# Merging the rest tiles, summing squares ahead of the router product, and re-timing GpSimd in an attention and expert kernel

## The chip, the cores and the metric

The kernel runs on one core of a Trainium2 chip. The metric is the device time of one launch in microseconds (us). The engines named here are TensorE (PE; its weight loads are the row PEld), VectorE (DVE), ScalarE (ACT), GpSimd (POOL) and SyncE (SP), which issues most transfers. Each engine works through its own list of instructions in order and waits on semaphores for the others.

## The reference, cut to what matters

Attention over 8 batches of 12 heads, 448 positions, head size 64, whose softmax has one more term in the denominator; then a router that sends each of the 448 tokens of a batch to one of 8 experts, and a two-layer expert.

```
scores = q @ k.T / sqrt(64);  m = max(scores);  e = exp(scores - m)
attn   = e / (sum(e) + exp(-m) + 1e-9);   attn_out = attn @ v
x      = attn_out, heads side by side                  # (8*448, 768)
xn, en = x / (norm(x) + 1e-6), expert_emb / (norm(expert_emb) + 1e-6)
logits = xn @ en.T / tau;  expert_idx = argmax(logits);  gate = softmax(logits)[expert_idx]
out    = gate * (relu(x @ w1[expert_idx]) @ w2[expert_idx])
```

## The kernel before: the parts that the change touches

The work is cut into 48 groups (six pairs of heads in each of eight batches). A group's 448 keys are three blocks of 128 and a "rest" of 64. The rests of the pair's two heads share one matmul. Every piece of work is put at a position; positions are sorted, and each engine gets its instructions in that order. A slot is 8 positions; group `g` begins at `8*g`. One slot thus mixes the scores of group `g`, the product with V of group `g-1`, the transposes for group `g+1`, and, once they run, two or three pieces ("chunks") of an expert of an earlier batch.

```python
LAG = 2 * NP                        # NP = 6; experts of batch b begin LAG groups after its first group
FILL = ((2.8, 5.3, 5.4), (2.8, 5.4))   # positions of expert chunks in even and odd slots, 15 a batch
...
def front_qk(k, g, s):              # transposes: q and k of a pair, one tile of two banks
    ps = k.big.tile([128, 2, 512], F32, name="big", tag="big")
    for m, x, r in ((0, t.qm, t.qr[...]), (1, t.km, t.kr[...])):
        for j in range(3):
            nc.tensor.transpose(ps[:, m, 128 * j : 128 * j + 128], x[:, j, ...], k.ident[:])
        nc.tensor.transpose(ps[:, m, SM:512], r, k.ident[:])      # the rest, one for q and one for k
    k.put(s + 1.1, k_out)           # ScalarE copies the 512 columns of k
    k.put(s + 2.1, q_out)           # VectorE copies the 448 columns of q
...
def scores(k, g, j, pa, pv):        # j = 0, 1, 2: a block of keys; j = 3: the rests, in a "work" tile
    ...                             # at pa: ScalarE takes exp; at pv: VectorE subtracts 1
def attend(k, g, s):                # product with V, in the one "av" tile: rests first, then 6 matmuls
    ...
    k.put(s + 2.3, recip)           # ScalarE: Ln, then Exp(-1 * .), gives 1 / denominator
def normalise(k, g, s): ...         # VectorE: x = (av + sum of v) * that
def square(k, g):                   # x*x: GpSimd for the first 11 groups, ScalarE after
    ...
def router_mm(k, b, s):             # 3 rounds of 4 column strips: 2 strips x@en, 2 strips sum of squares
    for r in range(3):
        for q in range(4): ...
def router_tok(k, b, s): ...        # 4 transposes of the router's result, in a "big" tile
...
    put(s + 1.2, lambda n=n: sum_v(k, n))                         # GpSimd: three adds every second group
    for j, o, pa, pv in ((0, 0, .3, 1.5), (1, .05, .4, 2.6), (2, 5.2, 6, 7.7), (3, .15, 2.6, 7)):
        put(s + o, lambda ...: scores(k, g, j, s + pa, s + pv))
    put(s + 8 + 0.1, lambda ...: attend(...)); put(s + 8 + 4.75, lambda ...: normalise(...))
    put(-NSLOT, lambda: warm(k, 24))                              # matmuls that keep TensorE busy at the start
...
n.work = pool("work", 2, space=PSUM)   # 2 tiles of one bank, taken in turn
n.big = pool("big", 2, space=PSUM)     # 2 tiles of two banks, taken in turn
n.av = pool("av", 1, space=PSUM)       # 1 tile of two banks
```

Expert chunks take "work" tiles as well: 8 of the hidden layer and 7 of the output, emptied by ScalarE or VectorE. After a batch's router, its most frequent expert is read into a register and GpSimd issues seven loads of that expert's weights.

Of the kernel before, what the change touches and what calls it, by code (L numbers as in the profile page):

```python
# [21 lines left out]
NP = H // 2  # L22
NF = F // 128
SM = 384
SR = S - SM
GP = 2
NG = 3
LAG = 2 * NP
FILL = ((2.8, 5.3, 5.4), (2.8, 5.4))
NSLOT = 8  # L30
# [6 lines left out]
def build_consts(k):  # L37
    nc, pool = k.nc, k.const
    nc.scalar.preload_act_table_set("natural_log_exp_and_others")
    k.ident = pool.tile([128, 128], F32, name="ident")  # L40
    make_identity(nc, k.ident[:])
    k.ones_f = pool.tile([128, 1], F32, name="ones_f")
    nc.vector.memset(k.ones_f[:], 1.0)
    iota_i = pool.tile([128, E], I32, name="iota_i")
    nc.gpsimd.iota(iota_i[:], pattern=[[1, E]], base=0, channel_multiplier=0)
    row_i = pool.tile([128, 1], I32, name="row_i")
    nc.gpsimd.iota(row_i[:], pattern=[[0, 1]], base=0, channel_multiplier=1)
    k.row = pool.tile([128, 1], F32, name="row")
    nc.vector.tensor_copy(out=k.row[:], in_=row_i[:])
    k.iota = pool.tile([128, E], F32, name="iota")  # L50
    nc.vector.tensor_copy(out=k.iota[:], in_=iota_i[:])

    k.vld, k.krest, k.qrest, k.vab = [], [], [], []
    for s in range(NG):
        v = pool.tile([128, 2 * GP, 4, DH], F32, name=f"vld{s}")
        nc.gpsimd.memset(v[:, :, 3, :], 0.0)
        k.vld.append(v)
        kr = pool.tile([128, GP, 128], F32, name=f"krest{s}")
        nc.vector.memset(kr[:], 0.0)
        k.krest.append(kr)  # L60
        qr = pool.tile([128, 2 * GP, DH], F32, name=f"qrest{s}")
        nc.gpsimd.memset(qr[64:128, :, :], 0.0)
        k.qrest.append(qr)
    for s in range(2):
        va = pool.tile([128, 4, 3, 64], F32R, name=f"vab{s}")
        nc.vector.tensor_copy(out=va[:, :, 1, :], in_=k.ones_f[:, 0:1].unsqueeze(2).broadcast_to([128, 4, 64]))
        k.vab.append(va)


# [66 lines left out]
def load_qk(k, n):  # L136

    nc = k.nc
    b, h0 = n // NG, n % NG * 2 * GP
    g0, s = h0 // 2, n % NG  # L140
    t = Net()
    t.qm = k.qkp.tile([128, 3, 2 * GP, DH], F32, name="qm", tag="qm")
    t.km = k.qkp.tile([128, 3, 2 * GP, DH], F32, name="km", tag="km")
    t.kr, t.qr, t.v = k.krest[s], k.qrest[s], k.vld[s]

    def rest2(src, two):
        return src[b].rearrange("(g two) s d -> two s g d", two=2)[two, SM:S, g0 : g0 + GP, :]

    keng = nc.sync if n else nc.scalar
    for eng, dst, src in ((nc.sync, t.qm, k.q), (keng, t.km, k.k)):  # L150
        for j in range(3):
            eng.dma_start(
                dst[:, j, :, :], src[b, h0 : h0 + 2 * GP, 0:SM, :].rearrange("h (p t) d -> t p h d", t=3)[j]
            )
    nc.sync.dma_start(t.qr[0:64, :, :], k.q[b, h0 : h0 + 2 * GP, SM:S, :].rearrange("h p d -> p h d"))
    keng.dma_start(t.kr[0:64, :, 0:64], rest2(k.k, 0))
    keng.dma_start(t.kr[64:128, :, 64:128], rest2(k.k, 1))
    k.ld[n] = t
# [14 lines left out]

def sum_v(k, n):

    nc, t = k.nc, k.ld[n]
    vs = k.vsp.tile([128, 2 * GP, DH], F32, name="vs", tag="vs")
    nc.gpsimd.tensor_tensor(out=vs[:], in0=t.v[:, :, 0, :], in1=t.v[:, :, 1, :], op=ALU.add)
    nc.gpsimd.tensor_tensor(out=vs[:], in0=vs[:], in1=t.v[:, :, 2, :], op=ALU.add)
    nc.gpsimd.tensor_tensor(out=vs[:], in0=vs[:], in1=t.v[:, :, 3, :], op=ALU.add)  # L180
    k.va[n] = vs


def front_qk(k, g, s):
    nc = k.nc
    n, i = g // GP, g % GP
    t = k.ld[n]
    ps = k.big.tile([128, 2, 512], F32, name="big", tag="big")
    for m, x, r in ((0, t.qm, t.qr[:, 2 * i : 2 * i + 2, :]), (1, t.km, t.kr[:, i, :])):
        for j in range(3):  # L190
            nc.tensor.transpose(ps[:, m, 128 * j : 128 * j + 128], x[:, j, 2 * i : 2 * i + 2, :], k.ident[:])  # L191
        nc.tensor.transpose(ps[:, m, SM:512], r, k.ident[:])  # L192
    def k_out():
        kt = k.qt.tile([128, 512], F32R, name="kt", tag="kt")
        nc.scalar.copy(out=kt[:], in_=ps[:, 1, :])  # L195
        k.kts[g] = kt

    def q_out():
        qt = k.qt.tile([128, S], F32R, name="qt", tag="qt")
        nc.vector.tensor_copy(out=qt[:], in_=ps[:, 0, 0:S])  # L200
        k.qts[g] = qt
    k.put(s + 1.1, k_out)
    k.put(s + 2.1, q_out)

# [9 lines left out]
def scores(k, g, j, pa, pv):  # L214
# [23 lines left out]
    def less_one(e):  # L238
        if j < 3:
            em = k.emp.tile([128, 2, S], F32R, name="em", tag="em")  # L240
            nc.vector.tensor_scalar_sub(em[:], e[:], 1.0)  # L241
        else:
            em = k.emp.tile([128, S], F32R, name="emx", tag="emx", bufs=2)
            nc.vector.tensor_scalar_sub(em[:], e[:, 0, :], 1.0)
        k.ems[g, j] = em
# [4 lines left out]
def attend(k, g, s):  # L250
# [4 lines left out]
    for h in range(2):  # L255
# [3 lines left out]
        )  # L259
    for j in range(3):  # L260
        for h in range(2):
            nc.tensor.matmul(  # L262
                ps[:, h, 0:S], lhsT=va[:, j, h : h + 2, :], rhs=k.ems[g, j][:, h, :],
                start=False, stop=(j == 2),
            )

    i = g % GP
    nc.tensor.matmul(ps[:, 0, S : S + 1], lhsT=k.va[g // GP][:, 2 * i : 2 * i + 2, :], rhs=k.ones_f[:], start=True, stop=True)  # L268
    rd = k.rdp.tile([128, 2, S], F32, name="rd", tag="rd")
    k.avs[g] = ps, rd  # L270

    def recip():
        nc.scalar.activation(rd[:], ps[:, :, 0:S], ACT.Ln, bias=1.0, scale=1.0 / (S + 1.0))  # L273
        nc.scalar.activation(rd[:], rd[:], ACT.Exp, scale=-1.0)  # L274

    k.put(s + 2.3, recip)

# [19 lines left out]


def square(k, g):
    x = k.xs[g]  # L300
    xs = k.xsp.tile([128, S], F32, name="xs", tag="xs")
    if g < LAG - 1:
        k.nc.gpsimd.tensor_tensor(out=xs[:], in0=x[:], in1=x[:], op=ALU.mult)  # L303
    else:
        k.nc.scalar.activation(xs[:], x[:], ACT.Square)
    k.xs[g] = (x, xs)


def router_mm(k, b, s):

    nc = k.nc
    ps = k.big.tile([128, 512], F32, name="rmm", tag="big")
    for r in range(3):
        for q in range(4):
            c = 3 * (q % 2) + r
            x = k.xs[b * NP + c][q // 2]
            nc.tensor.matmul(  # L317
                ps[32 * q : 32 * q + 32, 0:S], lhsT=(k.en[:, c, :] if q < 2 else k.ones32[:]), rhs=x[:],
                start=(r == 0), stop=(r == 2),
            )  # L320
# [5 lines left out]
def router_tok(k, b, s):  # L326

    nc, p = k.nc, k.rp
    tp = k.big.tile([128, 4, 128], F32, name="tok", tag="big")
    for t in range(4):  # L330
# [4 lines left out]
def router_logits(k, b, tp):  # L335

    nc, p = k.nc, k.rp
    nrm = p.tile([128, 4], F32, name="nrm", tag="nrm")
    nc.vector.reduce_sum(out=nrm[:], in_=tp[:, :, 64:128:32], axis=AX.X)  # L339
    l = p.tile([128, 4, E], F32, name="l", tag="l")  # L340
    nc.vector.reduce_sum(
        out=l[:], in_=tp[:, :, 0:64].rearrange("p t (q r) -> p t r q", q=2)[:, :, 0:E, :], axis=AX.X
    )
# [288 lines left out]
def pipeline(k):  # L632
# [6 lines left out]

    k.put = put  # L640
    put(4.6, lambda: build_late_consts(k))
    put(4, lambda: prep_expert_emb(k, 4))
    put(5 * NSLOT + 2.7, lambda: prep_expert_emb_t(k, 5 * NSLOT + 2.7))
    for n in range(NG * B):
        s = n * GP * NSLOT
        put(max(-NSLOT, s - 6 * NSLOT + 5.2), lambda n=n: load_qk(k, n))
        put(max(-NSLOT, s - 5 * NSLOT + 1.1), lambda n=n: load_v(k, n))
        put(s + 1.2, lambda n=n: sum_v(k, n))
    for g in range(G):
        s = g * NSLOT  # L650
        put(s - NSLOT + 4.2, lambda g=g, s=s - NSLOT + 4.2: front_qk(k, g, s))
        put(s + 0.8, lambda g=g: front_v(k, g))
        for j, o, pa, pv in ((0, 0, 0.3, 1.5), (1, 0.05, 0.4, 2.6), (2, 5.2, 6, 7.7), (3, 0.15, 2.6, 7)):
            put(s + o, lambda g=g, j=j, pa=s + pa, pv=s + pv: scores(k, g, j, pa, pv))
# [3 lines left out]
        put(s + 4.75, lambda g=g, s=s: normalise(k, g, s + 4.75))  # L658
        put(s + 7.1, lambda g=g: square(k, g))
    put(-NSLOT, lambda: warm(k, 24))  # L660
    for g in range(LAG):
        for o in (2.8, 5.4):
            put(g * NSLOT + o, lambda: warm(k, 3))
    for b in range(B):
        s = ((b + 1) * NP + 1) * NSLOT
        put(s + 2.75, lambda b=b, s=s: router_mm(k, b, s + 2.75))
        put(s + 7.9, lambda b=b, s=s: router_tok(k, b, s + 7.9))
        s += NSLOT
        put(s + 0.16, lambda b=b: router_pick(k, b))
        put(s + 0.9, lambda b=b: router_pow(k, b))  # L670
        put(s + 3.5, lambda b=b: router_count(k, b))
        put(s + 4.3, lambda b=b: router_index(k, b))
        for i, o in enumerate((4.4, 10, 16, 25, 31, 37, 43)):
            put(s + o, lambda b=b, i=i: fetch(k, b, i))
        put(s + 4.5, lambda b=b: router_exp(k, b))
        put(s + 7.2, lambda b=b: router_act(k, b))
        s += NSLOT
        put(s + 3.5, lambda b=b: keep_rows(k, b))
        put(s + 5.5, lambda b=b: keep_xb(k, b))
        put(s + 6, lambda b=b, s=s: router_gate(k, b, s + 6))  # L680

    late = {2.8: (4.7, False), 5.3: (7.3, True), 5.4: (8.5, True)}
    for b in range(B):
        pos = [((b * NP + LAG + i) * NSLOT, o) for i in range(NP) for o in FILL[i % 2]]
        for (s, o), fn in zip(pos, moe_chunks(k, b), strict=True):
# [7 lines left out]
def kernel(  # L693
# [35 lines left out]
    n.xp = pool("xp", 7)  # L729
    n.xsp = pool("xsp", 6)  # L730
    n.xbp = pool("xbp", 3)
# [3 lines left out]
    n.hp = pool("hp", 10)  # L735
    n.yp = pool("yp", 5)
    n.ld, n.qts, n.kts, n.ems, n.va, n.sv = {}, {}, {}, {}, {}, {}
# [40 lines left out]
```

The softmax here doesn't subtract the row's maximum and nothing guards it: scores larger than these inputs give would overflow.

## Time and profile before

| what | value |
|---|---|
| time, median of 3 | 430.42 us (430.19 to 431.25) |
| profiled span | 430.1 us |
| PE busy | 400.0 us (93%) |
| DVE busy | 314.8 us (73%) |
| ACT busy | 305.3 us (71%) |
| POOL busy | 171.7 us (40%) |
| matmuls | 2430 |

The shares are averages over three stages: attention alone, attention with experts, and the last two batches' experts alone. A row of a timeline has the start, the duration, the engine, the source line with the operation and its tiles, and in brackets how long the engine had been idle and what ended that. In the view of waits a line has the engine and what it wanted, what released it, and then the total, the count and the longest wait. An idle engine costs time only if the work that ends last hangs on it.

### The profile page before, as it was taken

The page shows a single profiled execution, that of the slowest core. Times are in us where ns is not written, and L with a number is a line of the kernel's source. Part 1 is how long each engine was busy: PE and PEld are TensorE (multiplying, and loading weights), DVE is VectorE, ACT ScalarE, POOL GpSimd, SP SyncE. Part 2 cuts the span into 40 slices and gives each one's busy share as a digit, 9 for nine tenths or more (in the row PEclk, how much of TensorE's full clock was granted, in tenths as well). Part 3 has the DMA queues.
Part 4 walks back from the last instruction along what each step waited for, and adds up shares of the span by engine and source line. Part 5 has one row for each costly group of instructions (what it writes and reads, how often), then busy time and mean ns, then how long its engine had stood idle before and what let it go on. Part 6 is the DMA issues. An engine that isn't in the chain of part 4 may idle for free.

```text
span 430.1 us, 7384 instructions
## 1 busy us (share of the span) xinstructions
PE 400.0 (93%) x2430; PEld 248.1 (58%) x2430; DVE 314.8 (73%) x658; ACT 305.3 (71%) x440; POOL 171.7 (40%) x242
## 2 busy tenths in 40 slices
PE   8878987879999999999999999999999999998885
PEld 3555554646556656665666656665666566644443
DVE  1697878789689769887787868976988778754222
ACT  1777776777788977978788878897698878751111
POOL 4043315754359106740377024910675037504500
PEclk9998999899999999999999999999999999999999
DMA  8775552997489964998399938997499508853973
GB/s 168 175 179 123 131 128 65 179 181 158 99 173 216 257 164 96 232 198 232 81 232 199 254 96 152 218 240 198 79 230 203 170 2 135 160 131 52 231 141 130
DMA packets 133690, 69.76 MB, mean 162 GB/s; under 512 B 99849, under 2 KB 127497, under 8 KB 133649
## 3 DMA queue, kind: packets, MB, share of 16 engines
q1 hardware_dynamic: 115392, 43.63, 40.0%
q0 software_dynamic: 16384, 25.17, 34.6%
q10 hardware_dynamic: 1872, 0.46, 0.6%
q8 instruction: 20, 0.33, 0.3%
q14 instruction: 22, 0.17, 0.1%
HBM read 83.39 MB, written 16.52 MB: 232 GB/s over the span
## 4 chain that ended last, share of the span: by engine, by line
PE 56%; DVE 20%; ACT 11%; issue 5%; POOL 4%; DMA 3%; POOLq 1%; DVEq 0%; ACTq 0%
PE av L262 11%; PE work L513 10%; PE work L485 8%; PE big L222 7%; DVE x L286 5%; PE big L191 4%; PE rmm L317 4%; DVE em L241 4%; DVE qt L200 4%; ACT e L233 3%; ACT rd L274 3%; DMA w<-in_moe_w_dram 3%; ACT rd L273 3%; PE work L629 2%; PE work L532 2%
## 5 line engine op out<-in xcount | busy, mean ns | idle before, releaser
L233 ACT ACTIVATE e<-big 128x896 f32<-128x896 f32 x144 | 127.6, 921 | 32.1 <-PE big L222 31.4
L241 DVE TENSOR_SCALAR em<-e 128x896 fp32r<-128x896 f32 x144 | 96.9, 687 | 7.2 <-ACT e L233 6.8
L286 DVE SCALAR_TENSOR_TENSOR x<-av,rd 64x448 f32<-64x448 f32 x96 | 66.3, 691 | 46.7 <-ACT rd L274 36.4
L485 PE MATMUL work<-xb,w 128*128 128x448 bf16 x384 | 79.7, 353 | 1.3 <-DMA w<-in_moe_w_dram 0.8
L262 PE MATMUL av<-em,vab 128*128 128x448 f32 x288 | 73.1, 391 | 0.0
L513 PE MATMUL work<-w,h 128*128 128x384 bf16 x384 | 68.4, 326 | 4.8 <-DMA w<-in_moe_w_dram 2.0
L222 PE MATMUL big<-qt,kt 64*128 64x448 f32 x288 | 56.8, 435 | 15.8 <-DVE qt L200 15.0
L357 POOL TENSOR_TENSOR nrm<-nrm,half 128x4 f32<-128x4 f32 x8 | 8.5, 1068 | 134.0 <-DVE nrm L339 134.0
L262 PEld LDWEIGHTS av<-em,vab 128*128 128x128 f32 x288 | 51.5, 192 | 16.2 <-issue 13.1
L485 PEld LDWEIGHTS <-w 128*128 128x128 bf16 x384 | 34.9, 98 | 39.4 <-issue 9.8
L273 ACT ACTIVATE rd<-av 128x896 f32<-128x896 f32 x48 | 44.1, 919 | 17.4 <-PE av L268 11.2
L445 POOL DMA_DIRECT2D w<-in_moe_w_dram x56 | 45.2, 809 | 27.0 <-issue 23.0
L513 PEld LDWEIGHTS <-h 128*128 128x128 bf16 x384 | 35.5, 98 | 31.5 <-issue 9.3
L222 PEld LDWEIGHTS big<-qt,kt 64*128 64x128 f32 x288 | 24.3, 184 | 43.1 <-ACT e L233 14.4
L200 DVE CAST qt<-big 128x448 fp32r<-128x448 f32 x48 | 29.9, 624 | 24.1 <-ACT kt L195 22.8
L274 ACT ACTIVATE rd<-rd 128x896 f32<-128x896 f32 x48 | 45.7, 952 | 1.5
L195 ACT CAST kt<-big 128x512 fp32r<-128x512 f32 x48 | 28.1, 585 | 12.1 <-PE big L192 12.0
L503 DVE TENSOR_SCALAR y<-work,g 128x384 f32<-128x384 f32 x32 | 19.6, 614 | 15.4 <-PE work L513 11.2
L629 PE MATMUL work<-ident 128*128 128x512 bf16 x96 | 28.6, 426 | 2.0 <-POOL ident masks.py:199 1.7
L493 DVE TENSOR_SCALAR h<-work 128x448 bf16<-128x448 f32 x40 | 24.6, 617 | 6.8 <-PE work L485 6.7
L209 DVE CAST vab<-vld 128x512 fp32r<-128x512 f32 x48 | 29.4, 612 | 0.0
L303 POOL TENSOR_TENSOR xs<-x 128x448 f32<-128x448 f32 x11 | 10.3, 933 | 40.5 <-DVE x L286 34.7
(103 smaller groups left out, 569.2 us busy)
## 6 DMA issues: line engine op xcount, KB each, us to landing
w<-in_moe_w_dram POOLq DMA_DIRECT2D x24, 512.0 KB, 7.9
w<-in_moe_w_dram POOLq DMA_DIRECT2D x32, 384.0 KB, 7.8
qm<-in_q_dram SPq DMA_DIRECT2D x72, 128.0 KB
vld<-in_v_dram SPq DMA_DIRECT2D x24, 384.0 KB
out_dram<-y SPq DMA_DIRECT2D x48, 192.0 KB
km<-in_k_dram SPq DMA_DIRECT2D x69, 128.0 KB
qrest<-in_q_dram SPq DMA_DIRECT2D x24, 64.0 KB
vld<-in_v_dram SPq DMA_DIRECT2D x48, 32.0 KB
```

What stands on the lines that cost most here:

```text
L200: nc.vector.tensor_copy(out=qt[:], in_=ps[:, 0, 0:S])
L222: nc.tensor.matmul(ps[:, h, 0:S], lhsT=kt[64 * h : 64 * h + 64, 128 * j : 128 * j + 128], rhs=qt[64 * h : 64 * h + 64, :], start=True, sto ...
L233: nc.scalar.activation(e[:], ps[:, :, 0:S], ACT.Exp, scale=scale)
L241: nc.vector.tensor_scalar_sub(em[:], e[:], 1.0)
L262: nc.tensor.matmul(ps[:, h, 0:S], lhsT=va[:, j, h : h + 2, :], rhs=k.ems[g, j][:, h, :], start=False, stop=(j == 2),)
L273: nc.scalar.activation(rd[:], ps[:, :, 0:S], ACT.Ln, bias=1.0, scale=1.0 / (S + 1.0))
L274: nc.scalar.activation(rd[:], rd[:], ACT.Exp, scale=-1.0)
L286: nc.vector.scalar_tensor_tensor(out=x[r, :], in0=ps[r, h, 0:S], scalar=ps[r, 0, S : S + 1], in1=rd[o, h, :], op0=ALU.add, op1=ALU.mult,)
L445: k.nc.gpsimd.dma_start(w[:], src)
L485: nc.tensor.matmul(ps[:, 0:S], lhsT=w1[c // 2][:, c % 2, 128 * f : 128 * f + 128], rhs=xb[:, c, :], start=(c == 0), stop=(c == NP - 1),)
L513: nc.tensor.matmul(ps[:, 0:SM], lhsT=hs[f][:, 128 * t : 128 * t + 128], rhs=w2[f // 2][:, f % 2, SM * n : SM * n + SM], start=(f == 0), st ...
L629: nc.tensor.matmul(ps[:], lhsT=idb[:, 0:128], rhs=idb.unsqueeze(1).broadcast_to([128, 2, 256]), start=True, stop=True)
```

## The change

It has five parts. (1) Merged rests: q's and k's rests lie in one tile and are transposed together, so a group has seven transposes and not eight. The q tile ("tq") stays in "big"; the k tile ("tk") moves to "work". VectorE copies q and the two halves of k's rest earlier in the slot, ahead of normalising; ScalarE copies 384 columns and not 512. (2) Summed squares: VectorE adds the squares of five groups, so the router product has two rounds and not three. (3) Timed GpSimd adds: GpSimd's squares and sums of v wait for VectorE's last subtraction, after which VectorE reads PSUM. (4) The rest scores come between the two parts of the product with V while there are no experts, and behind the product once experts run. (5) Timing: experts begin a slot earlier, with chunks placed 3, 3, 1, 2, 3, 3; the router's count, index, loads and exponential are re-placed; 18 warming matmuls and not 24.

```diff
-LAG = 2 * NP
-FILL = ((2.8, 5.3, 5.4), (2.8, 5.4))
+LAG = 2 * NP - 1
+FILL = 2 * ((2.8, 5.3, 5.4),) + ((2.8,), (2.8, 5.4)) + 2 * ((2.8, 5.3, 5.4),)
 ...
-    ps = k.big.tile([128, 2, 512], F32, name="big", tag="big")
+    pq = k.big.tile([128, 512], F32, name="tq", tag="big")
+    pk = k.work.tile([128, 512], F32, name="tk", tag="work")
 ...
-        nc.scalar.copy(out=kt[:], in_=ps[:, 1, :])
+        nc.scalar.copy(out=kt[:, 0:SM], in_=pk[:, 0:SM])
+    def r_out():
+        for h in range(2):
+            r = slice(64 * h, 64 * h + 64)
+            nc.vector.tensor_copy(out=kt[r, SM + 64 * h : S + 64 * h], in_=pq[r, S:512])
-    k.put(s + 2.1, q_out)
+    k.put(s + 0.5, q_out)
+    k.put(s + 0.5, r_out)
 ...
+    k.put(s + 0.04, rest)            # the six matmuls of the product, as a piece of their own
 ...
+def on_pool(g):
+    return g < LAG - 1 and g % NP < NP - 1
+def square_add(k, g):
+    acc = k.xs[g - g % NP][1]
+    k.nc.vector.tensor_tensor(out=acc[:], in0=acc[:], in1=k.xs[g][1][:], op=ALU.add)
 ...
-    for r in range(3):               # router_mm
+    for r in range(2):
 ...
-    tp = k.big.tile([128, 4, 128], F32, name="tok", tag="big")
+    tp = k.work.tile([128, 4, 128], F32, name="tok", tag="work")
 ...
-        put(s + 1.2, lambda n=n: sum_v(k, n))
+        put(s - NSLOT + 4.69, lambda n=n: sum_v(k, n, (1, 2)))
+        put(s + 4.69, lambda n=n: sum_v(k, n, (3,)))
 ...
-        for j, o, pa, pv in (..., (3, 0.15, 2.6, 7)):
+        rest = (3, 0.12, 2.3, 2.7) if g < LAG else (3, 0.15, 2.6, 7)
+        for j, o, pa, pv in (..., rest):
 ...
-        put(s + 7.1, lambda g=g: square(k, g))
-    put(-NSLOT, lambda: warm(k, 24))
+        put(s + NSLOT + (4.68 if on_pool(g) else 2.35), lambda g=g: square(k, g))
+        if 0 < g % NP < NP - 1:
+            put(s + 2 * NSLOT + 0.6, lambda g=g: square_add(k, g))
+    put(-NSLOT, lambda: warm(k, 18))
 ...
-        put(s + 3.5, lambda b=b: router_count(k, b))
-        put(s + 4.3, lambda b=b: router_index(k, b))
-        for i, o in enumerate((4.4, 10, 16, 25, 31, 37, 43)):
+        put(s + 6.9, lambda b=b: router_count(k, b))
+        put(s + 7.05, lambda b=b: router_index(k, b))
+        for i, o in enumerate((7.1, 10.5, 14, 20, 26, 32, 38)):
-        put(s + 4.5, lambda b=b: router_exp(k, b))
-        put(s + 7.2, lambda b=b: router_act(k, b))
+        put(s + 7.2, lambda b=b: router_exp(k, b))
+        put(s + 10.38, lambda b=b: router_act(k, b))
```

## The prediction

> **What bounds the kernel now.** I read the table of windows first, because the kernel has three stages. The columns are start and end, length, then busy time of PE, PEld, DVE, ACT and POOL.
>
> ```profile
> 14.00:60.80 46.80, 39.94 (x223) 26.15 (x224) 40.10 (x75) 36.96 (x51) 14.00 (x16) 0.96 0.62 148
> 201.24:248.08 46.84, 46.21 (x296) 29.46 (x299) 37.66 (x80) 38.43 (x57) 19.82 (x27) 1.00 0.89 194
> 383.86:430.10 46.24, 37.10 (x236) 19.52 (x235) 14.30 (x40) 7.24 (x14) 11.06 (x18) 1.00 0.60 129
> ```
>
> With experts beside attention TensorE is busy 46.21 of 46.84 us for a batch: it is the bound, at 7.81 us a slot. Before the experts no engine is full, so a loop of waits sets the slot. The early timeline shows which:
>
> ```profile
> 27.70 1.40 DVE L286 SCALAR_TENSOR_TENSOR x<-av,rd 64x448 f32<-64x448 f32 x2 [0.17 <-ACT rd L274]
> ...
> 29.13 0.62 DVE L200 CAST qt<-big 128x448 fp32r<-128x448 f32 x1
> ...
> 29.89 0.68 PE L222 MATMUL big<-qt,kt 64*128 64x448 f32 x4 [1.18 <-DVE qt L200]
> ...
> 30.40 1.73 ACT L233 ACTIVATE e<-big 128x896 f32<-128x896 f32 x2 [1.01 <-PE big L222]
> ```
>
> The next scores need qt, which stands behind x on VectorE, which waits for the reciprocal of the previous product. Score starts 23.20 and 29.89 give a slot of 6.69 us.
>
> For the mixed stage I read one slot's timeline in order. What matters is when the exponential of the rest scores ends:
>
> ```profile
> 371.80 0.68 PE L222 MATMUL big<-qt,kt 64*128 64x448 f32 x4
> ...
> 372.31 1.73 ACT L233 ACTIVATE e<-big 128x896 f32<-128x896 f32 x2 [1.65 <-PE big L222]
> ...
> 374.07 0.45 PE L228 MATMUL work<-qt,kt 128*128 128x448 f32 x1
> ...
> 374.24 0.92 ACT L273 ACTIVATE rd<-av 128x896 f32<-128x896 f32 x1 [0.20 <-PE av L268]
> ...
> 375.19 0.95 ACT L274 ACTIVATE rd<-rd 128x896 f32<-128x896 f32 x1
> 376.05 0.53 ACT L235 ACTIVATE e<-work 128x448 f32<-128x448 f32 x1
> ...
> 376.63 1.46 PE L513 MATMUL work<-w,h 128*128 128x384 bf16 x8 [0.40 <-ACT e L235]
> ```
>
> The exponential ends 4.78 us after the slot began, and the last row shows a chunk waiting for it, because the two "work" tiles are taken in turn. In this slot no transposes stood between; in ordinary slots 0.97 us of them do and the wait vanishes. Last, the chain of waits shows that the end hangs on the last expert's weights:
>
> ```profile
> 403.81 1.07 issue
> 404.90 12.34 DMA w<-in_moe_w_dram
> 417.28 1.78 PE work L513 x10
> ```
>
> [...] the 128x896 subtraction took 1.15 us at 23.58 beside a GpSimd add, and 0.61 us alone. [...]
>
> **The change part by part.** TensorE: a transpose less is 0.11 us a group (0.44 for four, by starts), 0.66 a batch; a router product of two rounds and not three is 2.39 x 1/3 = 0.80. So 46.84 - 1.46 = 45.4 a batch if nothing new waits, 7.56 a slot. ScalarE: 128 columns less, 0.11 us a group (slope 0.88 ns from 526 and 921 ns at 448 and 896). [...] Collisions avoided give back perhaps 1.5. So VectorE goes from 37.7 to about 41 a batch: near full, not the bound.
>
> Early stage: qt now stands ahead of x, so the loop above is cut. Per slot, as start-to-start times: ScalarE 3 x 0.86 + 0.48 + 0.95 + 0.86 + 0.42 = 5.3; VectorE 3 x 0.57 + 0.57 + 1.36 + 0.33 + 0.37 + 0.33 + 0.34 and 2/3 of an add = 5.4; TensorE with its warming 5.0. I take 5.8, plus 4.5 once for batch 0's router (product 1.6, transposes 0.5, and 2.2 for the two router waits worked out below). First product: at 17.42 before; six warming matmuls less (8.20/24 x 6 = 2.0) and a copy less in series give 15. So the product of group 10 stands at 15 + 58 + 4.5 = 77.5, while that of group 11 stood at 98.1 before.
>
> Mixed stage, where I expect the new wait. The k transposes now take a "work" tile. Five are taken per slot (rest scores, chunk, tk, chunk, chunk), two exist, so tk always follows the rest scores and must await their exponential. The square now stands on ScalarE ahead of the reciprocal. Laid out from the slot above: exponentials 0.51 to 2.24, square to 2.8, Ln from 2.75, Exp from 3.70, rest exponential 4.56 to 5.09, tk at 5.14. TensorE would reach tk at 2.57 + 1.15 (chunk) + 0.43 (tq) = 4.15. So it stands about 0.8 to 1.0 us, then goes on: tk 0.33, j2 scores 0.40, two chunks. A slot with three chunks takes 5.87 + 2 x 1.15 = 8.16 (hidden layer) or 5.87 + 2 x 1.36 = 8.59 (output). The slot with the router product hides the wait: 7.16. The slot after has two chunks, 7.3 if nothing else waits.
>
> Four three-chunk slots a batch, 2 x 8.16 + 2 x 8.59, with 7.16 and 7.3 make 48.0 us against 46.84 before. Beyond that, the router's one-hot reaches TensorE at about 3.3 in its slot, and Ln waits for that product: +0.7. The exponential of the logits stands ahead of Ln one slot later, and GpSimd's result for it comes 4.0 us after the index (213.18 to 217.22 before), which now follows x: +1.5. With both it is 50.2.
>
> From group 10 to 47 there are 37 slots, seven of 8.16 and six rounds of the other five: 57.1 + 6 x 39.8 = 296 without the router's waits, 57.1 + 6 x 42.0 = 309 with them.
>
> Tail: before, the last product ended at 380.15 and the kernel 49.95 later. Now it comes with four chunks ahead of the router product (4.6 us, about what x takes), product 1.6, copy and transposes 1.5, one-hot 1.95, index and load issue 2.4: first load at +12, against 392.78 - 380.15 = 12.6. Loads stand closer, so weights land some 2 us earlier: +47.7.
>
> Sum: 77.5 + 296 + 1.5 (that product) + 47.7 = 423 without the router's waits, 436 with all.
>
> **The rivals.** (A) No stall at tk: the slot falls to 7.56, 37 slots take 280, the end is at 406. For it speaks a full TensorE before; against it the 0.40 us wait that this same tile order already shows. (B) The stall and the router's waits both, 436: for it speaks this line, against it that every such wait lay hidden behind TensorE until now.
>
> ```profile
> ACT l L371 <- POOL l L365: 15.5, 8, 3.4
> ```
>
> (C) VectorE as the bound: it needs 41 us of 48, so waits at its in-order copies may add 0.2 a slot, 7 us. (D) The tail gains nothing because the weight transfers are limited by the DMA engines: +2.
>
> **Range and chances.** I weigh the stall alone (423) and the stall with the router's waits (436) about equally, and A at one in six: the mean is near 427. The early gain may be 5 us smaller or larger, a mixed slot's 0.2 us is worth 7: 413 to 439. Below 421.8 lies A and part of the first case: 0.30. Above 439.0: 0.10. Within 2%: 0.60.
>
> **What would show it.** In the changed profile: early score starts about 5.8 apart; TensorE idle at the tk transposes, ended by the rest exponential, some 0.8 us about 30 times; mixed batches of 48 to 50 us with TensorE no longer full; ScalarE waiting over 1 us for GpSimd's logits ahead of Ln; VectorE's subtractions at 0.62 throughout. Mixed batches of 45.4 would refute the stall, early slots above 6.5 the cut loop.

## The result and the profile after

The changed kernel takes 457.02 us (median of 4 runs, 456.53 to 457.43), the kernel before, measured beside it, 430.31 us. The ratio is 1.062, with a 95% interval of 1.0594 to 1.0646: slower by 6%, and 18 us above the top of the predicted range. Ratios here and below leave out runs over 1.5% above the fastest of their kernel. The profiled span is 455.6 us.

The windows of the kernel after (start and end, length, busy time of PE, PEld, DVE, ACT and POOL with counts, TensorE's clock, DMA share, GB/s), for the early stage from the first product, for one batch between two router products, and for the tail from the last product:

```profile
16.96:83.93 66.97, 60.62 (x327) 37.79 (x326) 55.91 (x135) 54.53 (x77) 29.61 (x39) 0.95 0.66 147
155.00:206.65 51.65, 46.07 (x281) 28.30 (x285) 40.04 (x95) 37.77 (x57) 18.83 (x27) 1.00 0.83 169
405.57:455.60 50.03, 38.44 (x230) 19.56 (x228) 15.37 (x41) 9.02 (x16) 11.06 (x18) 0.97 0.54 120
```

A batch grew from 46.84 to 51.65 us while TensorE's work in it did not grow (46.21 before, 46.07 now): it now idles 5.6 us a batch, and no other engine is near full (VectorE, the next, is busy for 40.04 of 51.65 us). That is a wait, not a load. The view of waits of the kernel after has these two. In the names, `e` is an exponential of scores, `em` the same after VectorE's subtraction (`emx` for the rests), `rd` the reciprocal, `xs` the square, `l` the router's logits:

```profile
PE tk L189 <- ACT e L242: 28.0, 30, 2.0
...
ACT l L390 <- POOL l L384: 16.1, 8, 3.3
```

The first line is the stall that the prediction laid out: the transposes of k wait for the exponential of the rest scores, 30 times. The second is hardly longer than in the kernel before (15.5 us in 8 waits there): GpSimd's logits are no later, but ScalarE's wait for them now holds up TensorE. An ordinary slot of the mixed stage shows how:

```profile
177.76 0.67 PE L229 MATMUL big<-qt,kt 64*128 64x448 f32 x4
...
179.89 0.58 ACT L320 ACTIVATE xs<-x 128x448 f32<-128x448 f32 x1
...
180.36 0.92 ACT L281 ACTIVATE rd<-av 128x896 f32<-128x896 f32 x1
...
181.31 0.95 ACT L282 ACTIVATE rd<-rd 128x896 f32<-128x896 f32 x1
...
182.17 0.52 ACT L242 ACTIVATE e<-work 128x448 f32<-128x448 f32 x1
...
182.74 0.55 PE L189 MATMUL tk<-ident,km 128*128 128x128 f32 x3 [0.51 <-ACT e L242]
...
186.33 0.66 PE L229 MATMUL big<-qt,kt 64*128 64x448 f32 x4
```

ScalarE does the square, Ln, Exp and only then the rest exponential; tk starts when that ends, at 4.98 us after the slot's first scores, and the slot takes 8.57 us. The slot before it is the worst of the batch, because the exponential of the router's logits (L390) stands ahead of Ln and waits for GpSimd:

```profile
171.29 0.24 POOL L384 TENSOR_TENSOR l<-l,nrm 128x32 f32<-128x32 f32 x1
...
171.56 0.23 ACT L390 ACTIVATE l<-l 128x32 f32<-128x32 f32 x1 [1.63 <-POOL l L384]
...
171.69 0.90 ACT L281 ACTIVATE rd<-av 128x896 f32<-128x896 f32 x1
...
173.48 0.53 ACT L242 ACTIVATE e<-work 128x448 f32<-128x448 f32 x1
...
174.06 0.55 PE L189 MATMUL tk<-ident,km 128*128 128x128 f32 x3 [1.98 <-ACT e L242]
```

GpSimd's lateness of 1.63 us is handed from ScalarE's queue to the rest exponential and from there to TensorE: that slot takes 10.54 us. The early stage did get faster, as intended; the timeline of the kernel after shows qt ahead of x, and score starts 5.81 us apart where they were 6.69:

```profile
26.62 0.47 PE L229 MATMUL big<-qt,kt 64*128 64x448 f32 x2
...
31.06 0.62 DVE L200 CAST qt<-tq 128x448 fp32r<-128x448 f32 x1 [0.54 <-PE tq L191]
...
32.08 1.40 DVE L295 SCALAR_TENSOR_TENSOR x<-av,rd 64x448 f32<-64x448 f32 x2
...
32.43 0.47 PE L229 MATMUL big<-qt,kt 64*128 64x448 f32 x2
```

The tail still hangs on the last expert's weights, now on its first-layer weights (L504 is the hidden layer's product). The chain of waits after (start, duration, what) has:

```profile
421.49 10.24 DMA w<-in_moe_w_dram
431.78 10.17 PE work L504 x44
```

### The profile page after: what moved, and what is told of

Read it like the earlier page. It is cut to its first block, busy times and chain, and to the rows that moved or that the text cites. A ratio compares the mean times of both kernels' runs of the same rounds, so it can differ in the third digit from the quotient of the medians.

```text
span 455.6 us, 7234 instructions
## 1 busy us (share of the span) xinstructions
PE 398.5 (87%) x2306; PEld 238.9 (52%) x2306; DVE 327.4 (72%) x787; ACT 301.0 (66%) x442; POOL 160.8 (35%) x237
## 4 chain that ended last, share of the span: by engine, by line
PE 48%; DVE 18%; ACT 14%; issue 8%; DMA 7%; POOL 4%; SPq 1%; POOLq 0%; ACTq 0%; DVEq 0%
PE work L504 11%; PE work L532 9%; PE av L273 8%; DVE x L295 6%; PE big L229 4%; ACT e L240 4%; ACT rd L281 4%; ACT e L242 3%; PE rmm L336 3%; PE tk L189 3%; PE work L551 3%; DVE qt L200 2%; DMA qm<-in_q_dram 2%; DMA w<-in_moe_w_dram 2%; POOL nrm L383 2%
## 5 line engine op out<-in xcount | busy, mean ns | idle before, releaser
L248 DVE TENSOR_SCALAR em<-e 128x896 fp32r<-128x896 f32 x144 | 86.3, 625 | 1.3 <-ACT e L240 1.1
L504 PE MATMUL work<-xb,w 128*128 128x448 bf16 x384 | 82.0, 359 | 5.8 <-DMA w<-in_moe_w_dram 4.6
L200 DVE CAST qt<-tq 128x448 fp32r<-128x448 f32 x48 | 30.0, 624 | 65.8 <-PE tq L191 65.7
L295 DVE SCALAR_TENSOR_TENSOR x<-av,rd 64x448 f32<-64x448 f32 x96 | 66.3, 691 | 12.1 <-ACT rd L282 10.1
L229 PE MATMUL big<-qt,kt 64*128 64x448 f32 x288 | 59.1, 446 | 6.5 <-ACT kt L196 3.5
L504 PEld LDWEIGHTS <-w 128*128 128x128 bf16 x384 | 34.9, 99 | 40.6 <-issue 6.5
L178 POOL TENSOR_TENSOR vs<-vs,vld 128x256 f32<-128x256 f32 x48 | 35.0, 730 | 48.6 <-issue 28.5
L178 POOL TENSOR_TENSOR vs<-vld 128x256 f32<-128x256 f32 x24 | 17.4, 726 | 93.6 <-PE work L235 75.1
L189 PE MATMUL tk<-ident,km 128*128 128x128 f32 x144 | 25.2, 284 | 28.0 <-ACT e L242 28.0
L522 DVE TENSOR_SCALAR y<-work,g 128x384 f32<-128x384 f32 x40 | 24.7, 616 | 22.7 <-PE work L532 11.0
L189 PEld LDWEIGHTS tk<-ident,km 128*128 128x128 f32 x144 | 15.7, 140 | 35.1 <-ACT e L242 35.1
L196 ACT CAST kt<-tk 128x384 fp32r<-128x384 f32 x48 | 22.9, 478 | 13.8 <-PE tk L189 13.7
L514 ACT ACTIVATE h<-work 128x448 bf16<-128x448 f32 x32 | 17.3, 540 | 19.1 <-PE work L504 19.1
```

Source lines behind the costliest of these rows:

```text
L178: k.behind(nc.gpsimd.tensor_tensor(out=vs[:], in0=(vs[:] if j > 1 else t.v[:, :, 0, :]), in1=t.v[:, :, j, :], op=ALU.add))
L189: nc.tensor.transpose(ps[:, 128 * j : 128 * j + 128], x[:, j, 2 * i : 2 * i + 2, :], k.ident[:])
L229: nc.tensor.matmul(ps[:, h, 0:S], lhsT=kt[64 * h : 64 * h + 64, 128 * j : 128 * j + 128], rhs=qt[64 * h : 64 * h + 64, :], start=True, sto ...
L248: k.last = nc.vector.tensor_scalar_sub(em[:], e[:], 1.0)
L295: nc.vector.scalar_tensor_tensor(out=x[r, :], in0=ps[r, h, 0:S], scalar=ps[r, 0, S : S + 1], in1=rd[o, h, :], op0=ALU.add, op1=ALU.mult,)
L504: nc.tensor.matmul(ps[:, 0:S], lhsT=w1[c // 2][:, c % 2, 128 * f : 128 * f + 128], rhs=xb[:, c, :], start=(c == 0), stop=(c == NP - 1),)
```

## The experiments

Two theories stood at the start. The first: the two waits named above, tk behind the rest exponential and ScalarE's queue behind the logits, make up the loss. The rival: a different part is at fault (VectorE's added copies, the square's place, the new fill), and the waits only show it. Each run is compared with the kernel before on the same chip; brackets hold the 95% interval of the ratio.

### 1. The rest scores ahead of the product in every slot

```diff
-rest = (3, 0.12, 2.3, 2.7) if g < LAG else (3, 0.15, 2.6, 7)
+rest = (3, 0.12, 2.3, 2.7)
```

The rest exponential then stands ahead of Ln on ScalarE, and tk need not wait for it.

> Theory (the k transposes wait in the 'work' tile for the exponential of the rest scores): with the rest scores ahead of the product in every slot, that exponential ends before Ln, about 2.8 us into the slot, so no wait is left at the tk transposes; slots with three chunks fall from 8.2 and 8.6 to about 7.6 and 8.0, the slot with the logits' exponential from 10.5 to about 8, and 37 mixed slots lose about 30 us: 420 to 430 us in all. Rival (VectorE, with 40 us of work a batch, or the later reciprocal is what holds the slot): the wait moves to VectorE's copies and the time stays within 8 us of 457.

Measured: 443.35 us, ratio 1.029 [1.021, 1.037]. The direction holds, 14 us came back, but it is between the two expectations, and about half of what the theory had. The tk wait is gone and another has come. In TensorE's timeline of this run, the second chunk of a slot waits for ScalarE to empty the first chunk's tile (L524):

```profile
172.48 1.83 PE L551 MATMUL work<-w,h 128*64 128x384 bf16 x16 [3.67 <-ACT y L524]
...
182.36 2.76 PE L532 MATMUL work<-w,h 128*128 128x384 bf16 x16 [0.35 <-ACT y L524]
```

The emptying stands behind Ln and Exp, so an ordinary slot loses 0.35 us; in the slot of the logits they stand behind L390, which waits for GpSimd, and the chunk loses 3.67 us here, 2.28 to 2.79 in the five other batches. With these takers of the two "work" tiles, moving one of them only chose which of them meets the late reader.

### 2. The square later, behind Ln

```diff
-put(s + NSLOT + (4.68 if on_pool(g) else 2.35), lambda g=g: square(k, g))
+put(s + NSLOT + (4.68 if on_pool(g) else 2.65), lambda g=g: square(k, g))
```

> Theory: the square on ScalarE delays Ln and so the rest exponential by 0.3 to 0.5 us. With the square behind that exponential, three slots a batch (those without a router's wait) start their tk transposes 0.3 to 0.5 us earlier: 3 x 0.3 to 0.5 x 6.2 batches = 6 to 9 us less, 448 to 451. Rival: another wait takes its place and the time stays at 457.

Measured: 462.47 us, ratio 1.073 [1.069, 1.077]: the opposite. In an ordinary slot the tk wait fell only from 0.51 to 0.36 us. So the square's place costs 0.15 us there, not its whole duration. In the slot of the router product it delays the sums of squares instead. The chain of waits of this run has

```profile
157.31 2.36 PE rmm L336 x16
```

where the kernel after spends 1.64 us. Three slots of a batch gain some 0.1 us each and the router product loses 0.72. So the square's place is not the cause of the loss.

### 3. The exponential of the logits later

```diff
-put(s + 10.38, lambda b=b: router_act(k, b))
+put(s + 13.45, lambda b=b: router_act(k, b))
```

> Theory: the exponential of the router's logits stands ahead of Ln and awaits GpSimd, which lengthens one slot a batch by about 1.9 us (10.54 against 8.57). Moved behind the copy of k, that slot falls to about 8.6 and batch 0's, still before the experts, by about 3: 6 x 1.9 + 3 = 14 us less, plus 1 to 2 us for the TensorE clock that falls after that idle time, about 442. Rival (the wait lies beside other waits): under 4 us less.

Measured: 443.36 us, ratio 1.027 [1.023, 1.032], as expected in all, though not in its parts. Batches fall from 51.7 to 50.1 us; two rounds in which TensorE's clock had fallen to 0.65 after this wait (see below) gain 1.7 us more each; and the product of group 10, which shows the early router, comes only 1.0 us earlier (82.88 against 83.86), where 3 had been expected. The tk waits stay: 18.2 us in 30, against 28.0. One ScalarE instruction of 0.23 us, put where its input is late, had cost 14 us.

### 4. In the kernel before: the k transposes alone in a "work" tile

```diff
-ps = k.big.tile([128, 2, 512], F32, name="big", tag="big")
+pq = k.big.tile([128, 512], F32, name="tq", tag="big")
+pk = k.work.tile([128, 512], F32, name="tk", tag="work")
```

Nothing else of the change is in it: eight transposes, three router rounds, old fill.

> The kernel before with one part alone: the k transposes in a 'work' tile, nothing else changed. Theory: the rest exponential ends 4.8 us into a slot, TensorE reaches the k transposes at about 4.3, so every mixed slot with experts loses 0.4 to 0.6 us less what slack it had: 36 slots, 10 to 20 us more than 430. Rival (the tile move is harmless by itself): 428 to 432.

Measured: 445.63 us, ratio 1.031 [1.027, 1.035], as expected. Batches go from 46.84 to 49.3 us, and the same wait stands in its timeline:

```profile
219.90 0.55 PE L192 MATMUL tk<-ident,km 128*128 128x128 f32 x3 [0.84 <-ACT e L236]
...
228.11 0.55 PE L192 MATMUL tk<-ident,km 128*128 128x128 f32 x3 [0.36 <-ACT e L236]
```

So the tile's move alone makes the kernel before 14 us slower (431.21 us beside it); this settles the first half of the first theory from the other side.

### 5. Experiments 1 and 3 together

> Rest scores ahead of the product in every slot, and the logits' exponential behind the copy of k. With the rest scores ahead alone, the second chunk of a slot waited for ScalarE to empty the first, behind Ln and Exp: 0.35 to 0.5 us in ordinary slots and 3.7 us in the slot of the logits' exponential. Theory: both waits of the 'work' tiles come from ScalarE's order, so the long one goes with the logits' wait and the batch falls from 50.2 to 47.0 or less: 415 to 424 us. Rival (the two edits remove the same wait): not below 435.

Measured: 422.78 us, ratio 0.977 [0.970, 0.985], as expected and faster than both kernels. Each alone gives 14 us, both give 34: they share ScalarE's queue, and while the logits hold it up, the rest scores' new place only hands the wait to the chunk (3.67 us). A batch is 46.53 us:

```profile
193.94:240.47 46.53, 44.57 (x281) 28.87 (x285) 40.05 (x95) 36.92 (x57) 18.90 (x28) 1.00 0.90 193
```

TensorE is near full again, with less work than before (44.57 us against 46.21). VectorE's 40.05 us did not prevent that, so its copies are not the cause either.

### 6. The k transposes in a second bank of q's "big" tile

```diff
-pq = k.big.tile([128, 512], F32, name="tq", tag="big")
-pk = k.work.tile([128, 512], F32, name="tk", tag="work")
+ps = k.big.tile([128, 2, 512], F32, name="tqk", tag="big")
+pq, pk = ps[:, 0, :], ps[:, 1, :]
```

Three runs: this alone; with the later logits of 3; and with both 3 and 1.

> The k transposes in the second bank of the q transposes' tile, which stands empty in the changed kernel; four 'work' tiles a slot, not five; rest scores where the change puts them. Theory: no wait at the k transposes, three-chunk slots 7.6 to 8.1, but the wait for the logits stays and now holds the second chunk: about 425 to 432. Rival (VectorE is the bound): above 445.

> As the last, with the logits' exponential behind the copy of k. Theory: TensorE is the bound again, a batch takes 45.4 to 46.5 us, and the changed early stage (83.9 us to the eleventh product, and some 5 less with the router's wait gone) is kept: 78 + 37 x 7.6 to 7.75 + 51.5 = 411 to 416, under both kernels. Rival (VectorE's 40 us a batch and its order hold the slot): batches of 48 or more, over 425.

> As the last, with the rest scores ahead of the product in every slot as well. Theory: with the k transposes out of the 'work' tiles the place of the rest scores hardly matters, within 4 us of the last; what differs is that Ln comes 0.5 us later in a slot.

Measured: 448.08 us, ratio 1.036 [1.024, 1.048]; ratio 1.014 [1.011, 1.017] for the second, whose single runs lay anywhere from 433.5 to 444.6 us (at a granted clock of 0.988 and 0.967); and 425.13 us, ratio 0.983 [0.974, 0.992]. All three missed: the first two are slower than their theories had it, and the third, expected within 4 us of the second, lies some 12 below it.

The mixed stage did gain: a batch takes 48.94 us in the first run, against 51.65 in the kernel after, and 45.5 in the third, the shortest of all, against 46.53 in experiment 5. The early stage lost: the first router product comes at 61.06 us in the first run and at 62.69 in the third, against 55.32 in the kernel after and 55.38 in experiment 5. The view of waits of the third says why:

```profile
ACT kt L196 <- DVE kt L206: 39.5, 47, 8.3
...
PE big L229 <- ACT kt L196: 12.9, 17, 2.2
```

ScalarE's copy of k now waits for VectorE's copies out of the same tile, where from two tiles they overlapped (in the kernel after, VectorE's copies of k's rest start at 31.60 us and ScalarE's copy at 31.78), and the next scores wait for the later one. Why the one waits for the other was not tested. Taking the k tile out of the rotation of "work" is thus no remedy in itself; the early stage pays for it.

### 7. Experiment 5 with the first chunk emptied by VectorE

```diff
-late = {2.8: (4.7, False), 5.3: (7.3, True), 5.4: (8.5, True)}
+late = {2.8: (4.7, True), 5.3: (7.3, False), 5.4: (8.5, True)}
```

> The best version so far (rest scores ahead of the product throughout, logits late), with one thing changed: the first chunk of each slot is emptied by VectorE and the second by ScalarE, instead of the other way round. If the 0.23 to 0.49 us that the second chunk waits for ScalarE to empty the first is what still separates its batches (46.5 us) from TensorE's work (44.6 to 45.4), the wait vanishes, batches fall to 45.4 to 46.0 us and the time to 415 to 419 us. Rival: VectorE, with 40 us of work in a batch of 46.5, is too full; the copy it gains ahead of x puts x and the next reciprocal back, batches stay at 46.5 or grow, and the time is 421 to 427 us.

Measured: 420.44 us (418.04 to 423.0), ratio 0.975 [0.968, 0.981]. Between the theories: batches came to 45.87 us as expected (one to 46.75), but the tail, which empties by the same rule, grew from 46.1 to 47.7 us after the last router product: GpSimd issued its first load 9.2 us after that product and not 6.6. The gain over experiment 5 is inside the intervals.

### 8. Experiment 5 with the experts' start and fill of the kernel before

```diff
-LAG = 2 * NP - 1
-FILL = 2 * ((2.8, 5.3, 5.4),) + ((2.8,), (2.8, 5.4)) + 2 * ((2.8, 5.3, 5.4),)
+LAG = 2 * NP
+FILL = 3 * ((2.8, 5.3, 5.4), (2.8, 5.4))
```

> The best version so far (rest scores ahead of the product throughout, logits late), with one part undone: experts begin at group 12 and not 11, and their chunks stand 3, 2, 3, 2, 3, 2 to the slots of a batch, as in the kernel before. If the earlier start is worth what TensorE does in it, three chunks (about 4 us) move from the attention's slots to the tail: 424 to 427 us, the end some 54 us after the last product and not 51.6. If an even spread suits the slots better than 3, 3, 1, 2, 3, 3, each batch gains back up to 0.5 us and the time stays within 2 us of 422.8.

Measured: 415.95 us, ratio 0.965 [0.962, 0.968], better than either theory had it. A batch falls from 46.53 to 45.87 us:

```profile
191.95:237.82 45.87, 44.22 (x281) 28.61 (x285) 39.70 (x95) 36.94 (x57) 19.18 (x28) 1.00 0.87 191
```

The last router product comes 4.3 us earlier (370.84 against 375.18), and the tail after it is 2.7 us shorter (43.5 against 46.1) although three chunks moved into it: TensorE waits there 0.91 us for first-layer and 1.28 us for second-layer weights, where it had waited 1.78 and 3.12 us, and the 44 matmuls after the last first-layer load take 8.50 us and not 9.99. So the earlier start and the fill of part 5 together cost some 7 us once the stalls are gone. (The constant also moves one square to GpSimd and adds warming matmuls to one slot; these were not separated.)

### 9. The last batch's weights issued closer together

In experiment 5 (first line of the diff), and in experiment 8 with the second weights earlier too (second line):

```diff
-for i, o in enumerate((7.1, 10.5, 14, 20, 26, 32, 38)):
+... (7.1, 7.11, 7.12, 20, 26, 32, 38) if b == B - 1 else (as before)
+... (7.1, 7.11, 7.12, 14, 14.1, 14.2, 14.3) if b == B - 1 else (as before)
```

> The best version so far (rest scores ahead of the product throughout, logits late), with one thing changed: for the last batch alone the three loads of the expert's first weights are issued one after another, not with GpSimd's other work between them (they were issued at 381.74, 384.63 and 385.60 us, and the last landed at 397.7, 12.1 us later). If the tail hangs on when the loads are issued, the third is issued about 2.3 us earlier, lands at about 394 to 395 and the time falls by 2 to 4 us, to 419 to 421. If it hangs on what the DMA engines move, the third lands within 1 us of where it did and the time is within 1 us of 422.8.

> The version with the experts' start and fill of before (415.95 us), with one thing changed: for the last batch the three loads of the first weights are issued one after another and the four of the second weights follow earlier. In its tail TensorE waited 0.91 us for a first-weights load at 390.72 and 1.28 us for a second-weights load at 401.48, and was otherwise busy from 376 us on. If issue is what those loads lack, both waits go and the time falls by about 2 us, to 413 to 415. If the DMA engines are what they lack, the first wait stays or grows, because the second weights now share the engines with the first, and the time is 416 us or more.

Measured: 419.38 us, ratio 0.975 [0.970, 0.979], as expected, though its interval overlaps that of experiment 5; and 415.46 us, ratio 0.964 [0.962, 0.966], no more than 0.5 us from experiment 8. The chain of waits of experiment 5 has the load on which its tail hangs, with its issue and how long it took to land:

```profile
385.60 12.06 DMA w<-in_moe_w_dram
```

In the chain of the first run here it is

```profile
382.91 11.58 DMA w<-in_moe_w_dram
```

Issued 2.7 us earlier, it landed 3.2 us earlier: here an earlier issue helped. In the chain of experiment 8 it is a load of the second weights:

```profile
390.17 11.27 DMA w<-in_moe_w_dram
```

and in that of the second run here

```profile
384.49 16.17 DMA w<-in_moe_w_dram
```

Issued 5.7 us earlier, it took 4.9 us longer and landed 0.8 us earlier. This run's window from the first load's issue to that landing has a DMA share of 0.98 (the number before the last):

```profile
377.66:400.70 23.04, 21.25 (x129) 11.57 (x126) 7.47 (x17) 3.66 (x8) 9.87 (x17) 1.00 0.98 198
```

In experiment 8 the share was 0.95 over the same stretch, so a load issued earlier found little free. That the DMA engines are the limit fits, but the share alone does not show it: in experiment 5, where an earlier issue did help, it is 0.9 or more too in the slice of its page from 389.7 to 400.2 us, in which the load landed.

## Why the prediction was wrong

The mechanism was right: the stall stands where it was laid out, and the router's waits add to it. Two steps failed. The first is the weighing: "I weigh the stall alone (423) and the stall with the router's waits (436) about equally, and A at one in six". The case with all waits was the one that came. But the range, up to 439, holds 436, so this alone would not have put the result outside. The second step did: the sum of that case, 436, is 20 us short. Term by term:

| term of the sum | predicted | measured |
|---|---|---|
| product of group 10 | 77.5 | 83.9 |
| 37 slots of the mixed stage | 309 (296 without the router's waits) | 320.2 |
| last product | 1.5 | 1.4 |
| tail | 47.7 | 50.0 |
| sum | 436 (423) | 455.6 |

**The stall at tk: right.** 30 waits against "about 30 times". In ordinary slots it is 0.5 to 0.7 us and not 0.8 to 1.0, but the slots that it sets are the laid-out ones: 8.57 us against 8.59 (output), 8.23 and 8.22 against 8.16 (hidden layer). Rival A, no stall at all, got a sixth of the weight, although the 0.40 us wait of the same tile order stood in the profile before; experiment 4 shows the stall in that very kernel once the tile is moved. That the matmuls behind tk start only after it was assumed in the layout; in the ordinary slot shown above they do, the next scores at 183.22 us, behind tk at 182.74.

**The router's waits: right in kind, not certain enough and too small.** They were counted half because "every such wait lay hidden behind TensorE until now". But the stall itself had just been shown to take that cover away: with tk waiting for ScalarE, whatever delays ScalarE delays TensorE. Given the stall, the second case followed from the first. The three slots concerned took 7.36, 8.75 and 10.54 us where the sum had 7.16, 8.0 and 10.1. A wait that the sum lacked is part of it: the rest product of the next slot waits 0.71 us for emx, which stands behind x, and x behind the q copy, which now waits for the router product. That makes 1.4 us a batch, 8.4 in six.

**The clock: not foreseen.** In two rounds of six the wait at tk was followed by slower matmuls. In the slot shown above, which waited 1.98 us at 174.06, the two chunks after it took 1.49 and 1.47 us. One batch later:

```profile
225.74 0.55 PE L189 MATMUL tk<-ident,km 128*128 128x128 f32 x3 [1.99 <-ACT e L242]
...
226.62 2.43 PE L551 MATMUL work<-w,h 128*64 128x384 bf16 x16
...
228.99 2.16 PE L532 MATMUL work<-w,h 128*128 128x384 bf16 x8
```

TensorE's granted clock is 0.65 from 226.22 to 231.08 us, and that slot takes 12.20 us and not 10.54; the same slot of the last round (382.92 to 387.78 us) is alike. Two times 1.7 us, with the 8.4 of the three slots, is more than the 11.2 us that the mixed stage is over; the last slot, shorter than laid out at 6.93 us, gives some back.

**The early stage: slot right, router wrong.** Four of the first six slots are 5.8 us as predicted, so cutting the loop was worth what it was to be. But the first product came at 16.8 us and not 15: q's transposes waited 1.60 us for a load of the merged rest tile. And the four slots with batch 0's router took 7.5 us more than four plain slots, not 4.5. Two of them in the timeline of the kernel after:

```profile
71.87 0.23 ACT L390 ACTIVATE l<-l 128x32 f32<-128x32 f32 x1 [3.32 <-POOL l L384]
...
74.31 1.56 PE L229 MATMUL big<-qt,kt 64*128 64x448 f32 x4 [2.96 <-ACT kt L196]
...
76.71 2.44 PE L273 MATMUL av<-em,vab 128*128 128x448 f32 x6
```

GpSimd's result is 3.32 us late (it was 3.35 us late in the kernel before). ScalarE's copy of k stands behind it, TensorE has no chunk to fill the gap, idles 2.96 us, and then six matmuls that took 1.42 us at 67.22 take 2.44. The other two of the first six slots took 6.7 and 6.4 us, 1.5 us too much; in both stands the one-time preparation of the expert embeddings, with VectorE's part of it ahead of the q copy in the first. That it is the cause was not tested. The three terms, 1.8, 3.0 and 1.5, make 6.3 of the 6.4 us.

**The tail: rival D had the outcome.** The first load was issued 12.05 us after the last product (predicted 12, before 12.6), and the third, on which TensorE then waits, 15.9 us after it, where it was 17.9 before. But this third load took 10.24 us to land where the third before took 7.8 (398.06 to 405.83 us), so it landed 0.5 us later than before, and nothing was gained. The wait for it had grown from 0.75 to 3.37 us, and after it the clock fell once more (0.66 from 431.78 to 436.80 us): 44 matmuls took 10.17 us, and 8.51 before. These 1.7 us are most of the 2.3 us by which the tail is over. D's reason, the DMA engines, stays open: the first run of experiment 9 gained by an earlier issue, the second hardly did.

**VectorE and the other costs: right.** 40.0 us a batch against 41, and experiment 5 speaks against rival C, VectorE as the bound. What the adds of squares and the small copies cost in that 41, and the adds in the early slot's 5.4 us, was the author's estimate, which no trace of before shows; in the kernel after they took 616 and 217 ns. The subtractions averaged 625 ns, and 687 before. Of those that stand alone in a row of the timeline before, 17 ran beside a GpSimd add or square and 12 of these took 0.96 to 1.16 us, the other five 0.62; 73 ran beside none and took 0.61 to 0.73. In the kernel after one such row is left beside a GpSimd add or square (1.18 us at 83.44), so most of this lengthening did go with the timed adds. The merged router product took 1.64 us against the expected 1.59. The square was one wrong term in the layout: it was to push the rest exponential back by about 0.3 us and pushes it by 0.15 (experiment 2).

**What stays open.** Why ScalarE's copy waits for VectorE's in experiment 6, why the place of the rest scores is worth 12 us there and what spreads its second run; which waits the clock follows; and whether the later start of experiment 8 helps as much with the waits still in place, which was not tried.

## What to carry to other kernels

When a tile moves into a pool whose buffers are taken in turn, write down the whole order of takers and ask which reader each must await; experiments 1 and 4 show the same wait at two takers. Once one engine waits for another's queue, a late input in that queue reaches it too, so two such terms are not alternatives to be averaged: they add up. Here GpSimd's 1.63 us at ScalarE made a wait of 1.98 us at TensorE, where ordinary slots have 0.5 to 0.7. Removing one alone can show less than it is worth: each of experiments 1 and 3 gave 14 us alone and 20.6 with the other in place. And a part of a change that looks bad with a stall in place may be good without it: with three placements altered (the rest scores, the logits, the start and fill) the rest of this change runs at 415.95 us, ratio 0.965, where the whole has 1.062.

## What the hardware showed that was not expected

TensorE's granted clock fell after some idle stretches and not after others of the same length. In the kernel after, the idle stretch ahead of 74.31 us is 2.96 us in the trace, and the slot after it ran at a granted clock of 0.63; of six waits of 1.98 to 2.02 us in the mixed stage, two were followed by a clock of 0.65 over 4.86 us and four by 1.00. In the kernel before, six matmuls at 37.87 us, 0.9 us after an idle stretch of 1.54 us, took 2.35 us at a clock of 0.57, where the six at 45.52 took 1.50. What decides it no run here shows.

In the kernel after, a GpSimd operation on four elements a partition (the power -1 of the router's norm) took 1.05 to 1.33 us, against 0.24 us for a multiplication on 32; it stands directly ahead of the logits. And the 512 KB weight load on which a tail hung took 10.24 us to land in the kernel after, where the median of such loads is 8.2, and 12.06 in experiment 5, where it is 9.3.
